# Attention and a gated feed-forward on one core: the softmax sums of 14 head pairs formed by accumulating transfers

## The chip, the cores and the metric

The kernel runs on one core of a Trainium2 chip. The time is the device time of one execution in microseconds, on that core; before the change it is 910.99 us, the median of three runs (910.42 to 911.65). TensorE (PE) does matrix products, VectorE (DVE) and ScalarE (ACT) work element by element, GpSimd (POOL) here clears two tiles and issues transfers, SyncE (SP) only issues transfers. SBUF is the on-chip memory of 128 partitions, PSUM the one that TensorE writes.

## The reference

Four batches of eight heads, 768 positions, head width 64. A query sees the keys with the same six hash bits; the result is laid out as 3,072 tokens of width 512 and goes through a feed-forward block of width 2,048.

```python
q_bits = (np.einsum('bhsd,dk->bhsk', q, proj) > 0)
k_bits = (np.einsum('bhsd,dk->bhsk', k, proj) > 0)
mask = q_bucket[:, :, :, None] == k_bucket[:, :, None, :]
scores = np.where(mask, scale * np.matmul(q, k.transpose(0, 1, 3, 2)), -1000000000.0)
attn = np.exp(scores - np.max(scores, axis=-1, keepdims=True))
attn = attn / (np.sum(attn, axis=-1, keepdims=True) + 1e-09)
x = np.matmul(attn, v)          # then (B,H,S,D) -> (B*S, H*D)
h = x @ w_in
g = h * erf(np.maximum(h, 0.0) + np.log1p(np.exp(-np.abs(h))))
out = g @ w_out
```

The sum over the keys in the fifth line is what the change treats. The weights w_in and w_out arrive as 64-bit floats, and the kernel makes 32-bit ones of them.

## The kernel before, in words

There are two stages. In the attention, two heads make a pair, so there are 16 pairs (i), each of two halves (h = 2i, 2i+1) of 384 queries. A half has six blocks of 128 keys. For a block, TensorE forms the scores of both heads with the keys on the partitions (`score`, L548: a product of hash bits that carries a large negative number where buckets differ, then q and k); ScalarE takes exp into `e_all` (L566), which holds nine blocks; TensorE multiplies by v (`weigh`, L629). Three PSUM tiles hold scores, so TensorE can be three blocks ahead of ScalarE.

The sum of e over the keys is made in two steps. VectorE adds the six blocks of a half (`sum_keys`, L617), in two wide rooms (`wide_sums`: x_sum and blocks[1], tiles that are free until the feed-forward), alternating by halves. That leaves 128 partial sums for each query, one on each partition. TensorE adds these with a matrix of ones (`divisor`, L664, tile z_ps), ScalarE copies the row out (`keep_divisor`, L677). For a pair, SP then sends z to DRAM and gets it back spread over the partitions (`spread`, `gather`), VectorE inverts it (`invert`), SP sends it out and broadcasts it back (`ungather`, `widen`, tile r), VectorE multiplies (`normalise`, L750), and SP stores the pair (`send`).

The hash bits of pair i are computed some pairs ahead: TensorE (`bits_of`, L817), sign on ScalarE (`sign_of`, L826), a weight on VectorE (`weigh_bits`, L836), and then POOL sends them to DRAM (`leave_bits`, L846) and, once they have landed, brings them into the layout that the scores need (`place_bits`, L855, two transfers).

Beside this the weights are converted, in 32 pieces of 128 x 512: POOL loads a piece of 512 KB (`fetch_weights`, L454, tile raw), ScalarE makes a mask of it (`square_high`, `keep_normal`), VectorE makes the high part (`move_bits`, `mask_bits`), the rest (`add_rest`, L522), and adds both (L530). Eight sums of weight blocks (`presum_weights`, L771, tile w_sum) prepare the feed-forward, which uses Strassen-like products.

The order of all this is made by a planner in the kernel, `arrange`. Each operation is given an engine, a cost, a rank, what must come before it (`after`), and `late`, the time from its end until another engine may count on it. The planner keeps a clock for each engine and emits, again and again, the operation that starts first, by rank. TensorE's order is a chain fixed by hand. The planner's clock sets the order only; at run time each engine works off its own list in that order, and waits on semaphores. An instruction that waits holds back all that stand behind it on its engine. In the planner before, what follows on the same engine is counted as ready when its predecessor ends, which for a transfer is when it was issued.

Of the kernel before, what the change touches and what calls it, by code (L numbers as in the profile page):

```python
# [54 lines left out]
F32 = mybir.dt.float32  # L55
BF16 = mybir.dt.bfloat16
I32 = mybir.dt.int32
# [6 lines left out]
P = 128  # L64
# [22 lines left out]
class Op:  # L87
# [11 lines left out]
    table: str = None  # L99
    late: float = 0.06  # L100


# [15 lines left out]
def arrange(ops, rooms, patience=0.0):  # L118
# [18 lines left out]
    def open_up(op):  # L137
        at = 0.0
        for a in op.after:
            if a in names:  # L140
                away = 0.0 if names[a].engine == op.engine else names[a].late
                at = max(at, ready[a] + away)
        open_ops[op.engine].append((op, at))
# [50 lines left out]
def kernel(  # L194
# [36 lines left out]
    QB = QR // 2  # L231
    WARM = 10
    proj_sb = const.tile([P, 2 * QR], F32, name="proj_sb")
    weight = const.tile([P, 2], F32, name="weight")
# [179 lines left out]
    def attention():  # L414
        NS = NPAIR * 4
        with (
# [10 lines left out]
            def big(name):  # L427
# [9 lines left out]
            raws = {}  # L437
            NH = NPAIR * 2
            wide_sums = [
                t.rearrange("p a b c -> p (a b c)")[:, 0 : 4 * HS].rearrange(  # L440
# [36 lines left out]
            def move_bits(n):  # L477
                if n not in raws:
                    return
                high = raws[n][:, :, 1]  # L480
                top = raws[n, "top"] = cvt.tile([P, WP], I32, name="top", tag="top")
# [16 lines left out]

            def mask_bits(n):
                if n not in raws:  # L500
                    return
                top = raws[n, "top"]
                unit = raws[n, "unit"] = cvt.tile([P, WP], I32, name="unit", tag="unit")
# [12 lines left out]
            def add_rest(n):  # L516
                if n not in raws:
                    return
                top, unit = raws.pop((n, "top")), raws.pop((n, "unit"))
                low = raws.pop(n)[:, :, 0]  # L520
                rest = cvt.tile([P, WP], F32, name="rest", tag="rest")
                nc.vector.scalar_tensor_tensor(  # L522
                    out=rest,
                    in0=low.bitcast(U32),
                    scalar=2.0**-52,
                    in1=unit[:, :].bitcast(F32),
                    op0=ALU.mult,
                    op1=ALU.mult,
                )
                nc.vector.tensor_tensor(  # L530
                    out=pieces[n][0], in0=top[:, :].bitcast(F32), in1=rest, op=ALU.add
                )
# [60 lines left out]
            def sum_keys(h, k):  # L593
                i, half = divmod(h, 2)
                d = pairs[i]
                if k == 0:
                    if h >= NH - 2:
                        if half:
                            room = blocks[1][:, :, :].rearrange("p k t -> p (k t)")[:, 0:S]
                        else:  # L600
                            room = load.tile([P, S], F32, name="q", tag="q")
                        d["sum", half] = room.rearrange("p (n a c) -> p n a c", n=1, a=2)
                    else:
                        d["sum", half] = wide_sums[h % 2]
                s = d["sum", half]
# [31 lines left out]
            def home(i, what):  # L637

                if i < NPAIR - 1:
                    shape, bufs = {"x": (S, 3), "z": (HS, 1), "r": (S, 2)}[what]  # L640
                    return xst.tile([P, shape], F32, name=what, tag=what, bufs=bufs)
# [48 lines left out]
            def leave_plain(i):  # L690
# [9 lines left out]
                )  # L700

            def spread(i):

# [25 lines left out]
            def ungather(i):  # L729
                d = pairs[i]  # L730
                rd = d["rd"] = dram.tile([2, 2, HS], F32, name="rd", tag="rd")
                nc.sync.dma_start(
                    out=rd.rearrange("h a c -> (h a c)").rearrange("(p c) -> p c", c=2 * S // P),
                    in_=d["zc"],
                )
# [108 lines left out]
            def leave_bits(i):  # L844
                bd = pairs[i]["bd"] = dram.tile([4, 2, QB, HS], BF16, name="bd", tag="bd")
                nc.gpsimd.dma_start(out=bd.rearrange("n a r c -> (n a r) c"), in_=sg)  # L846

            def place_bits(i):
# [30 lines left out]
            for h in range(NH):  # L879
# [3 lines left out]
                if h % 2 and (h + 3) // 2 < NPAIR:  # L883
                    order.append(("bits", (h + 3) // 2))
                if h >= 1:
                    order.append(("divisor", h - 1))
                order += [("weigh", 2 * h), ("weigh", 2 * h + 1)]
            slots = []
            for what, n in order:
# [12 lines left out]
                else:  # L902
                    h = n // 2
                    after = (("exponential", n, GC - 1),)
                    if n % 2 == 0:
                        after += (("leave", h - 1), ("leave_plain", (h - 1) // 2))
                    pe(weigh, (n,), 2.02, after)
            sums_after = {}
            for h in range(NH):
# [16 lines left out]
            for h in range(NH):  # L926
                for k, (blocks_, _, _, where) in enumerate(sum_steps(h)):
                    after = tuple(("exponential", 2 * h + b // GC, b % GC) for b in blocks_)
                    after += (("sum_keys", h, k - 1), ("sum_keys", h - 1, last_sum(h - 1)))
                    if k == 0:  # L930
                        after += (("divisor", h - 2),)
                        if h == NH - 2:
                            after += (("measure", NPAIR - 3, 0, 1),)
                    op(sum_keys, (h, k), "DVE", 1.72 if where == 2 else 0.92, (1, 2 * h + 1, k), after)
            for h in range(NH - 1):
                i = h // 2
# [8 lines left out]
            for h in range(NH):  # L945
                i = h // 2
                op(leave, (h,), "ACT", 0.48, (0, 2 * h, -2), (("weigh", 2 * h + 1), ("send", i - 3)))
                if h % 2 == 0:
                    op(leave_plain, (i,), "DVE", 0.15, (0, 2 * h, 0), (("weigh", 2 * h + 1),))
            for i in range(NPAIR):  # L950
                n = 4 * i
                if i:
# [38 lines left out]
                if i == NPAIR - 1:  # L991
                    continue
                op(spread, (i,), "SP", 0.4, (0, n, 0), (("keep_divisor", 2 * i + 1),), late=3.0)
                op(gather, (i,), "SP", 0.35, (0, n, 1), (("spread", i),), late=4.5)
                op(invert, (i,), "DVE", 0.4, (0, n + 8, 3), (("gather", i),))
                op(ungather, (i,), "SP", 0.35, (0, n, 2), (("invert", i),), late=3.0)
                op(
# [12 lines left out]
            for n in range(len(pieces)):  # L1010
# [13 lines left out]
                op(mask_bits, (n,), "DVE", 1.1, (2, n, 1), (("move_bits", n), ("keep_normal", n)), late=1.5)  # L1024
                op(add_rest, (n,), "DVE", 1.3, (2, n, 2), (("mask_bits", n),))
            for k in range(8):
                op(
                    presum_weights,
                    (k,),
                    "DVE",  # L1030
                    1.2,
                    (2, 31, k),
                    (("add_rest", 8 * (k // 4) + 7), ("presum_weights", k - 1)),
                )
            op(load_x, (0,), "SP", 1.1, (1, 0), (("send", JP - 1), ("start_pair", 10)), late=4.0)
# [748 lines left out]
```

## Time and profile before

The profiled execution took 910.96 us, of which its span, from the first to the last instruction, is 909.2; TensorE's granted clock was 0.999.

| stage, us from the start | length | PE busy | DVE busy | ACT busy | DMA share |
|---|---|---|---|---|---|
| 20 to 50 | 30 | 29.97 | 28.84 | 25.07 | 0.48 |
| 50 to 80 | 30 | 28.63 | 26.79 | 23.05 | 0.69 |
| 110 to 140 | 30 | 30.00 | 28.98 | 23.15 | 0.74 |
| 200 to 230 | 30 | 30.00 | 28.04 | 25.57 | 0.50 |
| 290 to 320 | 30 | 30.00 | 28.44 | 21.85 | 0.25 |
| 321.58 to 909.20 (feed-forward) | 587.62 | 581.42 | 380.35 | 317.75 | 0.20 |

Busy times are microseconds in that stretch; the DMA share is the mean busy share of the core's 16 DMA engines. Instructions that issue transfers aren't counted as busy on SP and ACT. A profile line such as "L664 PE MATMUL z_ps<-x,ones" names the line of the kernel, the engine, the operation, the tile written and those read.

### The profile page before, as it was taken

Reading aid. Unit: us, or ns where it says so; the run is one execution under the profiler, and the core shown is the slowest. Engines: PE = TensorE matmul, PEld = TensorE weight load, DVE = VectorE, ACT = ScalarE, POOL = GpSimd, SP = SyncE. Lnnn points to the kernel's source line nnn. Section 1 sums busy time; section 2 is a strip of 40 time slices with the busy share of each in tenths; the row PEclk is TensorE's granted clock in tenths of the full one; section 3 lists DMA queues with packets and bytes.
Section 4 is the critical chain, followed back from the end, with each engine's and each line's share of the span. In section 5 each row is a group of like instructions: output and inputs, shape, how many; then the busy total and the mean of one; then the engine's idle time right before and its main releaser. Section 6 shows DMA issues by size and latency. Waiting matters only on the chain.

```text
span 909.2 us, 12885 instructions
## 1 busy us (share of the span) xinstructions
PE 900.3 (99%) x5016; PEld 661.9 (73%) x5016; DVE 673.3 (74%) x863; ACT 571.9 (63%) x824; POOL 58.2 (6%) x95
## 2 busy tenths in 40 slices
PE   9999999999999999999999999999999999999997
PEld 5444444444444478888888888888888888888886
DVE  5989999989999969986566556756776556655653
ACT  6878887888887849755555545555655555545520
POOL 0211111111121000000000001000100000000000
PEclk9999999999999999999999999999999999999999
DMA  8455677656574231111122114211321023101321
GB/s 203 130 162 148 169 176 189 187 141 165 157 194 136 59 123 64 38 45 70 52 65 82 35 47 105 81 36 47 87 99 35 35 58 94 35 32 52 69 70 50
DMA packets 65013, 86.83 MB, mean 96 GB/s; under 512 B 34348, under 2 KB 47500, under 8 KB 64944
## 3 DMA queue, kind: packets, MB, share of 16 engines
q1 hardware_dynamic: 56384, 63.81, 24.6%
q0 software_dynamic: 8112, 21.66, 8.6%
q8 instruction: 41, 0.67, 0.3%
q10 hardware_dynamic: 448, 0.46, 0.2%
q14 instruction: 28, 0.23, 0.1%
HBM read 64.67 MB, written 17.30 MB: 90 GB/s over the span
## 4 chain that ended last, share of the span: by engine, by line
PE 92%; issue 1%; DMA 1%; ACT 0%; POOL 0%; DVE 0%; DVEq 0%; ACTq 0%; POOLq 0%
PE M L1317 32%; PE X L1204 28%; PE st L548 14%; PE av L629 12%; PE M L1204 3%; PE z_ps L664 1%; PE bits L817 1%; DMA raw<-in_w_in_dram 0%; POOL both L855 0%; ACT e_all L566 0%; ACT keep L468 0%; DMA bd<-sg 0%; DVE u L1352 0%; ACT x L688 0%; DVEq L1727 0%
## 5 line engine op out<-in xcount | busy, mean ns | idle before, releaser
L1244 DVE SCALAR_TENSOR_TENSOR e<-w,e 128x1024 f32<-128x1024 f32 x144 | 173.8, 1221 | 8.9 <-ACT w L1238 4.2
L566 ACT ACTIVATE e_all<-st 128x768 f32<-128x768 f32 x192 | 150.9, 813 | 11.9 <-PE st L548 11.5
L1238 ACT ACTIVATE w<-h,cq 128x1024 f32<-128x1024 f32 x144 | 155.6, 1137 | 0.2 <-DVE e L1244 0.2
L548 PE MATMUL st<-q,k 64*128 64x384 f32 x768 | 155.0, 483 | 0.0
L1226 DVE TENSOR_TENSOR h<-X,h 128x512 f32<-128x512 f32 x65 | 44.8, 689 | 146.0 <-PE X L1204 145.8
L1317 PE MATMUL M<-w_out_sb,h 128*128 128x256 f32 x576 | 141.5, 379 | 0.0
L629 PE MATMUL av<-e_all,v 128*64 128x385 f32 (+1 forms) x768 | 131.1, 490 | 0.0
L1204 PE MATMUL X<-x,w_in_sb 128*128 128x256 f32 x512 | 121.0, 379 | 0.0
L1317 PEld LDWEIGHTS M<-w_out_sb,h 128*128 128x128 f32 x576 | 109.4, 190 | 14.9
L1222 ACT COPY h<-X 128x512 f32<-128x512 f32 x85 | 49.3, 580 | 112.4 <-PE X L1204 112.3
L1234 ACT ACTIVATE e<-h,cq 128x1024 f32<-128x1024 f32 x48 | 55.2, 1150 | 82.7 <-DVE h L1226 82.7
L1204 PEld LDWEIGHTS X<-x,w_in_sb 128*128 128x128 f32 x512 | 97.3, 190 | 13.2
L629 PEld LDWEIGHTS av<-e_all,v 128*64 128x64 f32 x768 | 52.4, 136 | 67.2 <-issue 65.2
L1317 PE MATMUL M<-wt,S 128*128 128x256 f32 x384 | 95.6, 379 | 0.0
L548 PEld LDWEIGHTS st<-q,k 64*128 64x128 f32 x768 | 68.2, 188 | 34.9 <-issue 34.2
L1204 PE MATMUL X<-x_sum,w_sum 128*128 128x256 f32 x344 | 81.3, 379 | 0.0
L1317 PEld LDWEIGHTS M<-wt,S 128*128 128x128 f32 x384 | 73.0, 190 | 9.9
L1204 PEld LDWEIGHTS X<-x_sum,w_sum 128*128 128x128 f32 x344 | 65.4, 190 | 8.9
L548 PE MATMUL st<-both 64*128 64x384 bf16 x384 | 62.9, 324 | 1.6 <-ACT e_all L566 1.4
L1259 DVE TENSOR_TENSOR h<-h,e 128x1024 f32<-128x1024 f32 x48 | 58.0, 1221 | 3.7 <-ACT e L1255 3.6
L1255 ACT ACTIVATE e<-e 128x1024 f32<-128x1024 f32 x48 | 50.4, 1054 | 7.8 <-DVE e L1244 7.4
L548 PEld LDWEIGHTS <-both 64*128 64x128 bf16 x384 | 19.5, 94 | 43.1 <-issue 21.2
(126 smaller groups left out, 1073.4 us busy)
## 6 DMA issues: line engine op xcount, KB each, us to landing
wt<-wt SPq DMA_DIRECT2D x24, 768.0 KB, 4.2
raw<-in_w_out_dram POOLq DMA_DIRECT2D x16, 512.0 KB, 4.6
raw<-in_w_in_dram POOLq DMA_DIRECT2D x14, 512.0 KB, 4.3
v<-in_v_dram SPq DMA_DIRECT2D x32, 192.0 KB, 4.8
xs<-x SPq DMA_DIRECT2D x16, 384.0 KB, 3.1
q<-in_qkT_dram SPq DMA_DIRECT2D x30, 192.0 KB, 4.2
k<-in_qkT_dram SPq DMA_DIRECT2D x30, 192.0 KB, 4.4
r<-rd SPq DMA_DIRECT2D x30, 192.0 KB, 3.4
```

Source lines behind the costliest of these rows:

```text
L548: nc.tensor.matmul(out=st[:, ab, 0:HS], lhsT=d["k" + src][rows, keys], rhs=d["q" + src][rows, cols], start=(part == 0), stop=(part == 1),)
L566: nc.scalar.activation(out=e[:, :, 0:HS], in_=st[:, :, 0:HS], func=AF.Exp, scale=scale)
L629: nc.tensor.matmul(out=d["av"][rows, 0:w], lhsT=d["v"][:, g * GC + c, rows], rhs=e[:, ab, 0:w], start=(g == 0 and c == 0), stop=(g == 1 an ...
L1204: nc.tensor.matmul(out=d[where][:, u, :], lhsT=a[:, kc, f : f + P], rhs=b[:, kc, :], start=(first and u == 0 and kc == 0), stop=(last and ...
L1222: nc.scalar.copy(out=quarter(p, q), in_=st[p][where])
L1226: nc.vector.tensor_tensor(out=h, in0=st[p][where], in1=h, op=ALU.add)
L1234: nc.scalar.activation(out=s, in_=unit(p, v), func=AF.Sigmoid, bias=cq[:, n : n + 1])
L1238: nc.scalar.activation(out=q, in_=unit(p, v), func=AF.Sigmoid, scale=GATE_S[j][0], bias=cq[:, j : j + 1])
L1244: nc.vector.scalar_tensor_tensor(out=s, in0=st[p].pop(("q", v, j)), scalar=GATE_S[j][2], in1=s, op0=ALU.add, op1=ALU.mult,)
L1255: nc.scalar.activation(out=s, in_=s, func=AF.Tanh, scale=GATE_LEAD)
L1259: nc.vector.tensor_tensor(out=h, in0=h, in1=st[p].pop(("s", v)), op=ALU.mult)
L1317: nc.tensor.matmul(out=banks[name][:, sub, :], lhsT=a[:, u, sub * P : (sub + 1) * P], rhs=b[:, u, :], start=(c == 0 and k == 0), stop=(c = ...
```

## The change

For the first 14 pairs (`FOLDED`), z no longer goes through TensorE. VectorE's last sum of each half writes into one of three rooms, `pair_sums` (parts of blocks[1] and of w_sum), both halves of a pair beside each other. POOL then issues three accumulating transfers one after another (`fold`): rows 64 to 127 are added to rows 0 to 63, then 32 to 63 to 0 to 31, then 16 to 31 to 0 to 15. SP stores the 16 rows that are left (`spread_folded`) and brings them back with 16 values beside each other (`gather_folded`, tile zr), VectorE adds these 16 and inverts (`invert_folded`). The last two pairs go the old way.

The new field `far` makes the planner count `late` for followers on the same engine too, so it leaves 6.0 us between one fold's issue and the next. The last addition of a weight piece also becomes an accumulating transfer of POOL's (`complete_weights`). The bits' transfers are issued by ScalarE. The weight sums that write into w_sum wait until pair_sums no longer need that room. The old z path's own tile goes, its stored pairs get four buffers instead of three.

```diff
-                away = 0.0 if names[a].engine == op.engine else names[a].late
+                near = names[a].engine == op.engine and not names[a].far
+                away = 0.0 if near else names[a].late
...
+            FOLDED = NPAIR - 2
+            pair_sums = [
+                t.rearrange("p a b -> p (a b)")[:, 0 : 2 * S]
+                for t in (blocks[1][:, :, :], w_sum[:, 2, :, :], w_sum[:, 1, :, :])
+            ]
...
             def add_rest(n):
...
                 nc.vector.scalar_tensor_tensor(
-                    out=rest,
+                    out=unit,
                     in0=low.bitcast(U32),
                     scalar=2.0**-52,
-                    in1=unit[:, :].bitcast(F32),
+                    in1=unit,
                     op0=ALU.mult,
                     op1=ALU.mult,
                 )
-                nc.vector.tensor_tensor(
-                    out=pieces[n][0], in0=top[:, :].bitcast(F32), in1=rest, op=ALU.add
+
+            def complete_weights(n):
+
+                if (n, "unit") not in raws:
+                    return
+                nc.gpsimd.dma_start(
+                    out=pieces[n][0],
+                    in_=raws.pop((n, "unit"))[:, :].bitcast(F32),
+                    accum_op=ALU.add,
                 )
...
+                if i < FOLDED and k == last_sum(h):
+                    into = pair_sums[i % 3][:, half * S : (half + 1) * S].rearrange(
+                        "p (n a c) -> p n a c", n=1, a=2
+                    )
...
+            def fold(i, k):
+
+                n = P >> (k + 1)
+                s = pair_sums[i % 3]
+                nc.gpsimd.dma_start(out=s[0:n, :], in_=s[n : 2 * n, :], accum_op=ALU.add)
...
+            def spread_folded(i):
+
+                zf = pairs[i]["zf"] = dram.tile([ROWS, 2 * S], F32, name="zf", tag="zf")
+                nc.sync.dma_start(out=zf, in_=pair_sums[i % 3][0:ROWS, :])
+
+            def gather_folded(i):
+                d = pairs[i]
+                zr = d["zr"] = small.tile([D, ROWS, 2 * S // D], F32, name="zr", tag="zr", bufs=1)
+                nc.sync.dma_start(
+                    out=zr, in_=d.pop("zf").rearrange("r (p c) -> p r c", c=2 * S // D)
+                )
+
+            def invert_folded(i):
+                d = pairs[i]
+                zc = d["zc"] = small.tile([D, 2 * S // D], F32, name="zc2", tag="zc2")
+                nc.vector.tensor_reduce(
+                    out=zc, in_=d.pop("zr").rearrange("p r c -> p c r"), axis=AX.X, op=ALU.add
+                )
...
             def leave_bits(i):
                 bd = pairs[i]["bd"] = dram.tile([4, 2, QB, HS], BF16, name="bd", tag="bd")
-                nc.gpsimd.dma_start(out=bd.rearrange("n a r c -> (n a r) c"), in_=sg)
+                nc.scalar.dma_start(out=bd.rearrange("n a r c -> (n a r) c"), in_=sg)
...
-                    nc.gpsimd.dma_start(
+                    nc.scalar.dma_start(
                         out=both[i % 2][ab * D : ab * D + NBIT + 1, :, :].rearrange(
...
-                if h >= 1:
+                if h - 1 >= 2 * FOLDED:
                     order.append(("divisor", h - 1))
...
-                op(leave, (h,), "ACT", 0.48, (0, 2 * h, -2), (("weigh", 2 * h + 1), ("send", i - 3)))
+                op(leave, (h,), "ACT", 0.48, (0, 2 * h, -2), (("weigh", 2 * h + 1), ("send", i - 4)))
...
-                        op(leave_bits, (i,), "POOL", 0.7, (0, n - 6, 2), (("weigh_bits", i),), late=3.6)
+                        op(leave_bits, (i,), "ACT", 0.65, (0, n - 6, 2), (("weigh_bits", i),), late=5.0, far=True)
                         op(
                             place_bits,
                             (i,),
-                            "POOL",
-                            1.2,
+                            "ACT",
+                            1.25,
                             (0, n - 6, 3),
                             (("leave_bits", i), ("score", n - 5, 2), ("clean", i - 2)),
-                            late=3.6,
+                            late=4.5,
                         )
...
+                if i < FOLDED:
+                    for k in range(FOLDS):
+                        before = ("fold", i, k - 1) if k else ("sum_keys", 2 * i + 1, last_sum(2 * i + 1))
+                        op(fold, (i, k), "POOL", 0.9, (0, n, 4 + k), (before,), late=LATE, far=True)
+                    op(spread_folded, (i,), "SP", 0.4, (0, n, 0), (("fold", i, FOLDS - 1),), late=3.0, far=True)
+                    op(gather_folded, (i,), "SP", 0.35, (0, n, 1), (("spread_folded", i),), late=4.5, far=True)
+                    inverse = invert_folded
+                    op(inverse, (i,), "DVE", 0.7, (0, n + 8, 3), (("gather_folded", i),))
...
-                op(add_rest, (n,), "DVE", 1.3, (2, n, 2), (("mask_bits", n),))
+                op(add_rest, (n,), "DVE", 0.7, (2, n, 2), (("mask_bits", n), ("complete_weights", n - 2)))
+                op(complete_weights, (n,), "POOL", 0.9, (0, n, 1), (("add_rest", n),), late=5.5)
+            before = ()
+            for n, k in enumerate((0, 1, 2, 4, 5, 6, 3, 7)):
+                after = tuple(("complete_weights", 8 * (k // 4) + m) for m in range(8))
+                if k % 2:
+                    after += (("spread_folded", FOLDED - (1 if k % 4 == 3 else 3)),)
+                op(presum_weights, (k,), "DVE", 1.2, (2, 31, n), after + before)
+                before = (("presum_weights", k),)
```

More of the change, by code (lines that the diff above doesn't have):

```diff
@@ L100 @@
     late: float = 0.06
+    far: bool = False
 TABLE_LOAD = 1.28
@@ L232 @@
     WARM = 10
+    FOLDS = 3
     proj_sb = const.tile([P, 2 * QR], F32, name="proj_sb")
@@ L480, in move_bits @@
                 high = raws[n][:, :, 1]
-                top = raws[n, "top"] = cvt.tile([P, WP], I32, name="top", tag="top")
+                top = raws[n, "top"] = pieces[n][0].bitcast(I32)
                 nc.vector.tensor_scalar(
@@ L502, in mask_bits @@
                 top = raws[n, "top"]
-                unit = raws[n, "unit"] = cvt.tile([P, WP], I32, name="unit", tag="unit")
+                unit = raws[n, "unit"] = cvt.tile([P, WP], I32, name="unit", tag="unit", bufs=2)
                 nc.vector.scalar_tensor_tensor(
@@ L518, in add_rest @@
                     return
-                top, unit = raws.pop((n, "top")), raws.pop((n, "unit"))
+                raws.pop((n, "top"))
+                unit = raws[n, "unit"][:, :].bitcast(F32)
                 low = raws.pop(n)[:, :, 0]
-                rest = cvt.tile([P, WP], F32, name="rest", tag="rest")
                 nc.vector.scalar_tensor_tensor(
-                    out=rest,
+                    out=unit,
                     in0=low.bitcast(U32),
                     scalar=2.0**-52,
-                    in1=unit[:, :].bitcast(F32),
+                    in1=unit,
                     op0=ALU.mult,
@@ L603, in sum_keys @@
                     else:
-                        d["sum", half] = wide_sums[h % 2]
+                        d["sum", half] = wide_sums[h % 2 if i >= FOLDED else 0]
                 s = d["sum", half]
@@ L639, in home @@
                 if i < NPAIR - 1:
-                    shape, bufs = {"x": (S, 3), "z": (HS, 1), "r": (S, 2)}[what]
-                    return xst.tile([P, shape], F32, name=what, tag=what, bufs=bufs)
+                    if what == "z":
+                        return x_sum[:, :, :, :].rearrange("p a b c -> p (a b c)")[:, S : S + HS]
+                    return xst.tile([P, S], F32, name=what, tag=what, bufs={"x": 4, "r": 2}[what])
                 rows = blocks[1][:, :, :].rearrange("p k t -> p (k t)")
@@ L700, in leave_plain @@
                 )
+            def fold(i, k):
+                n = P >> (k + 1)
+                s = pair_sums[i % 3]
+                nc.gpsimd.dma_start(out=s[0:n, :], in_=s[n : 2 * n, :], accum_op=ALU.add)
+            ROWS = P >> FOLDS
+            LATE = 6.0
+            def spread_folded(i):
[13 more added lines that the diff above has]
+                )
+                nc.vector.tensor_scalar(
+                    out=zc, in0=zc, scalar1=S * EPS, scalar2=None, op0=ALU.add
+                )
+                nc.vector.reciprocal(out=zc, in_=zc)
             def spread(i):
@@ L732, in ungather @@
                 nc.sync.dma_start(
-                    out=rd.rearrange("h a c -> (h a c)").rearrange("(p c) -> p c", c=2 * S // P),
+                    out=rd.rearrange("h a c -> (h a c)").rearrange(
+                        "(p c) -> p c", c=2 * S // (D if i < FOLDED else P)
+                    ),
                     in_=d["zc"],
@@ L907, in attention, with i_of @@
                     pe(weigh, (n,), 2.02, after)
+            def i_of(h):
+                return h // 2
             sums_after = {}
@@ L930, in attention @@
                     if k == 0:
-                        after += (("divisor", h - 2),)
+                        if h == NH - 3:
+                            after += (("spread_folded", FOLDED - 2),)
+                        if h - 2 >= 2 * FOLDED:
+                            after += (("divisor", h - 2),)
                         if h == NH - 2:
                             after += (("measure", NPAIR - 3, 0, 1),)
+                    if k == last_sum(h) and i_of(h) < FOLDED:
+                        after += (("spread_folded", i_of(h) - 3),)
                     op(sum_keys, (h, k), "DVE", 1.72 if where == 2 else 0.92, (1, 2 * h + 1, k), after)
-            for h in range(NH - 1):
+            for h in range(2 * FOLDED, NH - 1):
                 i = h // 2
@@ L992, in attention @@
                     continue
[L993 to L996, printed above, removed]
+                if i < FOLDED:
[6 more added lines that the diff above has]
+                    op(inverse, (i,), "DVE", 0.7, (0, n + 8, 3), (("gather_folded", i),))
+                else:
+                    op(spread, (i,), "SP", 0.4, (0, n, 0), (("keep_divisor", 2 * i + 1),), late=3.0, far=True)
+                    op(gather, (i,), "SP", 0.35, (0, n, 1), (("spread", i),), late=4.5, far=True)
+                    inverse = invert
+                    op(inverse, (i,), "DVE", 0.4, (0, n + 8, 3), (("gather", i),))
+                op(ungather, (i,), "SP", 0.35, (0, n, 2), ((inverse.__name__, i),), late=3.0, far=True)
                 op(
@@ L1024, in attention @@
                 op(mask_bits, (n,), "DVE", 1.1, (2, n, 1), (("move_bits", n), ("keep_normal", n)), late=1.5)
-                op(add_rest, (n,), "DVE", 1.3, (2, n, 2), (("mask_bits", n),))
[L1026 to L1034, printed above, removed]
+                op(add_rest, (n,), "DVE", 0.7, (2, n, 2), (("mask_bits", n), ("complete_weights", n - 2)))
[7 more added lines that the diff above has]
+                before = (("presum_weights", k),)
             op(load_x, (0,), "SP", 1.1, (1, 0), (("send", JP - 1), ("start_pair", 10)), late=4.0)
```

## The prediction, made before the change was run

> **What bounds the kernel now.** I read the page first (busy shares, the 40 slices), then the chain of waits over one pair, then the busy time by stage, then the tiles of the hash bits.
>
> ```profile
> PE 900.3 (99%) x5016; PEld 661.9 (73%) x5016; DVE 673.3 (74%) x863; ACT 571.9 (63%) x824; POOL 58.2 (6%) x95
> PE   9999999999999999999999999999999999999997
> DVE  5989999989999969986566556756776556655653
> ACT  6878887888887849755555545555655555545520
> DMA  8455677656574231111122114211321023101321
> ```
>
> TensorE is busy for all but 9 us. In the first 14 slices (22.7 us each), the attention, VectorE and ScalarE are nearly full too and the DMA digits stand at 4 to 8; after that three of the four have room. So the attention is the stage to argue from, and it ends where the first feed-forward matmul starts, at 321.58 us in the chain. One pair of heads in that chain:
>
> ```profile
> 90.94 4.95 PE st L548 x36
> 95.89 0.46 PE z_ps L664 x8
> 96.36 4.03 PE av L629 x24
> 100.39 4.95 PE st L548 x36
> 105.34 0.78 PE bits L817 x8
> 106.12 0.33 PE z_ps L664 x8
> 106.45 4.02 PE av L629 x24
> 110.47 4.95 PE st L548 x36
> ```
>
> From 90.94 to 110.47 is 19.53 us a pair, with no hole: 2 x (4.95 + 4.02), 0.78 for the bits, and 0.46 + 0.33 for the two z products, which the change takes out. The same stretch, ten pairs long, by engine:
>
> ```profile
> core 0: us, PE busy (x) PEld busy (x) DVE busy (x) ACT busy (x) POOL busy (x), PEclk, DMA share, GB/s
> 80.86:276.15 195.29, 195.29 (x1442) 90.86 (x1444) 183.98 (x245) 158.52 (x290) 28.31 (x50) 1.00 0.64 169
> 112.00:114.00 2.00, 2.00 (x18) 1.25 (x16) 1.97 (x4) 2.00 (x4) 0.42 (x1) 1.00 0.98 261
> ```
>
> The reader is to see three reserves. DVE: 18.40 us of 19.53, practically none. ACT: 15.85 of 19.53. DMA: 0.64 x 19.53 = 12.5 us of all 16 engines a pair; in the loads' burst (the last row) it is already full, at 261 GB/s.
>
> **What the Trainium skill says.** "DMA: Bandwidth & Descriptors", section "SWDGE vs HWDGE vs iDMA": only GpSimd can issue an accumulating transfer, so folds and weight sums share POOL's queue with the weight loads. The trace agrees as far as it goes: its only accumulating transfers (u<-part, w<-part) are POOL's. The same page, "Issuing engines are not separate DMA queues": transfers issued by SP, ACT and POOL run on the same 16 engines. So moving the bits' transfers to ScalarE frees POOL's time and not a byte of bandwidth. The burst row above fits that: SP's loads and POOL's transfers together reach 0.98. "VectorE: DVE Perf Modes", section "The perf-mode tier table": tensor_reduce has only the 1x mode; no row here shows one.
>
> **The change part by part**, against the profiled run's own 910.96 us (span 909.2 and 1.8 around it); the median of 910.99 is the same number.
>
> *z off TensorE (28 of 32 halves).* Removes 0.46 + 0.33 = 0.79 us a pair; if a z beside the bits costs the full 0.46, 0.92. 14 pairs: 11.1 to 12.9, taken 12. The path is TensorE without a hole, so this comes through whole unless something else ends a wait. What would be late next are the DMA, ScalarE and VectorE, below.
>
> *z off ScalarE.* Two copies z<-z_ps at 0.33: 0.65 a pair, off the path.
>
> *VectorE.* Goes: one of the three-instruction finish of a weight piece, L530 at 0.692, two pieces a pair: 1.38. Comes: a reduce of 64x384 read elements, bounded by a 384-wide bf16 multiply (0.32) and a 512-wide f32 add (0.69), taken 0.5, and 0.05 for the wider reciprocal. Net -0.8. Seven of the eight weight presums (1.22 each) wait until pair_sums leave w_sum, so 8.5 us go from the middle to the last five halves: 18.40 - 0.8 - 1.0 = 16.6 a pair in the middle, while the last 20 us (19.41 of 20.48 busy) get fuller. Covered by the first 30 us of the feed-forward, where DVE has 7.6 us free; without that cover up to 5 us at its start.
>
> *New DMA work.* An accumulating 256 KB transfer has its price in the feed-forward:
>
> ```profile
> 555.60:561.50 5.90, 5.90 (x29) 5.20 (x28) 5.19 (x7) 2.13 (x4) 1.72 (x2) 1.00 0.66 133
> 561.60:567.00 5.40, 5.40 (x26) 4.75 (x25) 0.23 (x1) 0.59 (x1) 0.00 (x0) 1.00 0.29 97
> ```
>
> The second row holds 512 KB of plain stores: 0.29 x 5.4 = 1.57 us of 16 engines, 0.78 per 256 KB. The first holds one such store and two accumulations: 0.66 x 5.9 = 3.89, less 0.78, halved: 1.55 us each, twice the plain price. Per pair the change adds two weight sums (3.1), folds of 384 + 192 + 96 KB (2.6 x 1.55 = 4.1), zf of 96 KB (0.3), and zr, 1,024 rows of 96 bytes, of which no row shows the like (0.3 by bytes, perhaps 1; taken 0.6), less 0.1 for zd and zc: 8.0. With today's 12.5 that is **20.5 us of DMA a pair, where TensorE would need only 18.7**. 12.5 is measured in crowded bursts. At a quiet load's rate (a stretch from 106 to 108 us, raw alone, shows 0.65 at 224 GB/s, so 345 per full share) the 169 GB/s x 19.53 us = 3.3 MB cost 9.6, and the sum is 17.6. So 17.6 to 20.5, middle 19.0; the loads have deadlines, and I let the engines be used to 0.95: 20.1 us a pair.
>
> *POOL.* Goes: bits 0.55 + 2 x 0.58. Comes: five accumulations at 0.85 to 1.0. About +3 us a pair of 28.31/10; not the bound. But a fold waits in POOL's queue for the fold before, planned 6.0 us, and behind it stand the weight loads and sums. One transfer of 256 KB landed in 3.8 to 5.2 us on an idle DMA; the first fold is larger and goes off while the next pair's loads do. If it takes longer than 6.0, raw is late, and ScalarE waits for raw in order. The z path gets longer by some 20 us of planned time; four x buffers (74 us of pairs) hold that.
>
> *The bits on ScalarE.* Three issues a pair: 0.34 (SP's rows) to 0.6 (ACT's first loads, 1.20 for two): 1.0 to 1.8, taken 1.4. New are ScalarE's own waits: leave_bits for VectorE's weighed bits, place_bits for the landing.
>
> ```profile
> L826 ACT ACTIVATE sg<-bits,sgn x14: 586/591/638, 26.7 to 282.1; 128x384 bf16<-128x384 f32 x14
> L836 DVE TENSOR_SCALAR sg<-sg,weight_q x14: 319/320/321, 28.8 to 284.9; 64x384 bf16<-64x384 bf16 x14
>   POOL bd L846: 82.2, 14
> DMA to landing us min/median/max: 1.9/3.5/6.4
> ```
>
> POOL waited 82.2 us for these bits and nobody minded, for POOL had nothing behind them. Behind ScalarE stand the exps. In the timelines VectorE finishes the bits 1.6 to 4.6 us after the sign (mean 3.4), mostly since it works off its queue late. What ScalarE does in between is copies and squares, so its wait is between 0 and 3.4 a pair; VectorE's own relief shortens it, taken 1. The landing is planned at 5.0, median 3.5, longest 6.4: mostly covered now, less in a fuller DMA. ScalarE: 15.85 - 0.65 + 1.4 + 1 = 17.6 of 18.7 to 20.1. It fits on average; at the 20.1 us a pair that the DMA sets it has 2.5 us to spare.
>
> **Sum.** 14 pairs from 19.53 to 20.1 us: +8; the rest as before: 910.96 + 8 = **919 us**.
>
> **The rivals.**
> - *A, the forecast: the 16 DMA engines become the bound*, 919. For it: 20.5 against 18.7, and that the chain of z now has eight transfers, all in the crowd. Against: bursts are smoothed by three load buffers and 6 us between a load's landing and its use.
> - *B, the other side: the transfers stay under cover.* Place: the same DMA engines; price: 17.6 us a pair at quiet rates, under TensorE's 18.7; it decides from a DMA share under about 0.95 on, with ScalarE's bits waits within its 3.7 us of idle time. Then only z's removal counts: 910.96 - 12 = 899. For it: TensorE ran without a hole through 30 us stretches of 0.74.
> - *C, ScalarE's in-order waits replace the removed z.* Wait 2 us, issues 1.4, copies -0.65: 2.75 more a pair, in the weigh phase that already has no ScalarE idle time (0.21 us before the copy of av, against 2.37 in the other half). The three score banks absorb some 0.7; TensorE loses 2.0: 18.7 + 2.0 = 20.7, 14 x 1.2 = +17: 928. Against: VectorE is relieved.
> - *D, gain and stalls cancel*: 911. For it: the middle of the DMA sum, 19.0, with some waits, is 19.5.
>
> **How the numbers follow.** A 0.36, B 0.34, C 0.22, D 0.08. What can be told from no change is about 0.2%, 1.8 us. Faster 0.34 (B), same 0.08 (D), slower 0.58 (A and C). The range: low end B with a small rest of stalls at its ideal, 898; high end beyond C with some of A's crowding, 934. A alone: 912 (19.6 us a pair) to 927 (20.7).
>
> **What would show it.** Right: DMA share in the attention above 0.9, pairs at about 20 us, holes in TensorE before scores or bits whose releaser is a transfer (bits, loads) or an exp behind raw; fold landings above 6 us. Wrong: share below 0.85 and st to st in 18.7 us (B); or ACT waits of 2 us at leave_bits with a half-empty DMA (C). A feed-forward longer than its 587.6 us would say that the moved presums weren't covered, which no case here holds.

## The result, and the profile after

The changed kernel takes 977.12 us (median of four runs, 975.22 to 981.23), where the kernel before took 910.80 in the same comparison: a ratio of 1.0733, with a 95% interval of 1.0697 to 1.0769. The forecast was 919 with a range from 898 to 934: slower is right, the size is not.

The page of the profiled execution (981.23 us, span 979.4), its busy shares and slices of 24.5 us:

```profile
PE 914.6 (93%) x4792; PEld 669.3 (68%) x4792; DVE 667.2 (68%) x845; ACT 559.0 (57%) x796; POOL 97.2 (10%) x127
PE   9998878887979896999999999999999999999997
DVE  5886765776678689799766656665566566666653
ACT  6876654655666583596555555555555556555630
PEclk9999998898989999899999999999999999999999
DMA  7888876798879765211113201320132013001311
```

TensorE has 224 instructions less and yet holes in the attention; VectorE and ScalarE, nearly full before, have room now; the DMA digits stand mostly at 7 to 9 as far as the attention goes. No engine is full there and the transfers nearly are, which suggests that engines wait for landings; the waits below show it.

By stages: the first feed-forward matmul starts at 382.46 us, where it stood at 321.51, so 61 of the span's 70.2 us are lost in the attention. From there to the end it is 596.9 us against 587.7: 9.2 more. In the other cut, TensorE is idle for 64.8 us instead of 8.9 (span less busy), and busy for 14.3 more although z's products went: the score products take 171.7 + 70.0 us instead of 155.0 + 62.9, at a granted clock of 0.84 to 0.94 in most 30 us stretches with holes. Their larger group, before and after:

```profile
L548 PE MATMUL st<-q,k 64*128 64x384 f32 x768 | 155.0, 483 | 0.0
```

```profile
L563 PE MATMUL st<-q,k 64*128 64x384 f32 x768 | 171.7, 525 | 0.0
```

The Trainium skill ("TensorE: Matmul & The Clock Gate", "Part 1: The HAM clock gate") says why: "the default state is throttled, and activity releases the throttle". Both the holes and the lower clock in their stretches are in the trace. In the pair shown below, the clock reads 0.50 from 147 to 151 us, right after a hole of 4.68 us, and 1.00 from 152 us on; the scores of a block take 1.60 us there instead of 0.81. The products with v, which come later in a pair, take what they took (131.6 us, before 131.1). By these numbers the lower clock added about 24 us of slower products to the 56 us more of holes.

Who waited for whom, in the changed kernel's list of waits (total, times, longest):

```profile
ACT junk L669 <- DVE sg L891: 55.6, 14, 7.8
POOL w_sum L726 <- DMA w_sum<-w_sum: 53.1, 12, 7.3
PE st L563 <- ACT e_all L581: 43.2, 19, 6.1
DVE zc L747 <- DMA zr<-zf: 37.9, 11, 7.1
```

Read from the bottom up, it is one story, and one pair shows it in the timeline. VectorE:

```profile
131.30 1.75 DVE L636 TENSOR_TENSOR x_sum<-e_all 128x1536 f32<-128x1536 f32 x1
138.47 1.09 DVE L747 TENSOR_REDUCE zc<-zr 64x24 f32<-64x384 f32 x1 [5.42 <-DMA zr<-zf]
139.60 0.17 DVE L750 TENSOR_SCALAR zc<-zc 64x24 f32<-64x24 f32 x1
139.81 0.29 DVE L753 RECIPROCAL zc<-zc 64x24 f32<-64x24 f32 x1
140.03 1.69 DVE L636 TENSOR_TENSOR x_sum<-x_sum,e_all 128x1536 f32<-128x1536 f32 x1
141.75 0.96 DVE L636 TENSOR_TENSOR w_sum<-x_sum 128x768 f32<-128x768 f32 x1
142.74 0.32 DVE L891 TENSOR_SCALAR sg<-sg,weight_q 64x384 bf16<-64x384 bf16 x1
```

ScalarE in the same stretch:

```profile
137.01 0.51 ACT L669 ACTIVATE junk<-q 128x384 bf16<-128x384 f32 x1
137.42 0.19 ACT L669 ACTIVATION_READ_ACCUMULATOR junk<-q 128x1 f32 x1
143.09 0.35 ACTq L901 DMA_DIRECT2D bd<-sg  x1
143.49 0.52 ACT L669 ACTIVATE junk<-q 128x384 bf16<-128x384 f32 x1 [5.88 <-DVE sg L891]
```

And TensorE:

```profile
141.59 0.81 PE L563 MATMUL st<-q,k 64*128 64x384 f32 x4
147.09 0.50 PE L563 MATMUL st<-both 64*128 64x384 bf16 x2 [4.68 <-ACT e_all L581]
```

The inversion of an earlier pair stands in VectorE's list and its zr is still on its way: 5.42 us. Behind it are two sums and then this pair's weighed bits. ScalarE has come to leave_bits, which issues these bits, and stands for 5.88 us. Behind leave_bits are the copy of av and the next exps. TensorE fills its three banks of scores and stands for 4.68. A landing that is 5 us late is paid by three engines in turn, and in this pair comes out as a hole of almost the same length. Before the change VectorE waited 2.0 us for zc in the whole execution.

### The profile page after: what moved, and what is told of

Read it like the earlier page. It is cut to its first block, busy times and chain, and to the rows that moved or that the text cites. A ratio compares the mean times of both kernels' runs of the same rounds, so it can differ in the third digit from the quotient of the medians.

```text
span 979.4 us, 12421 instructions
## 1 busy us (share of the span) xinstructions
PE 914.6 (93%) x4792; PEld 669.3 (68%) x4792; DVE 667.2 (68%) x845; ACT 559.0 (57%) x796; POOL 97.2 (10%) x127
## 4 chain that ended last, share of the span: by engine, by line
PE 68%; DMA 16%; DVE 7%; issue 3%; ACT 2%; SPq 2%; POOL 0%; ACTq 0%; DVEq 0%; POOLq 0%
PE M L1389 30%; PE X L1276 26%; DMA zr<-zf 6%; PE st L563 4%; PE M L1276 4%; DMA zf<-w_sum 3%; PE av L648 3%; DVE x_sum L636 3%; DMA zf<-x 2%; DMA r<-rd 2%; DVE zc L747 1%; DMA w_in_sb<-unit 1%; DMA w_sum<-w_sum 1%; ACT e_all L581 1%; SPq L364 1%
## 5 line engine op out<-in xcount | busy, mean ns | idle before, releaser
L581 ACT ACTIVATE e_all<-st 128x768 f32<-128x768 f32 x192 | 145.2, 815 | 49.4 <-DMA q<-in_qkT_dram 12.7
L563 PE MATMUL st<-q,k 64*128 64x384 f32 x768 | 171.7, 525 | 0.0
L648 PE MATMUL av<-e_all,v 128*64 128x385 f32 (+1 forms) x768 | 131.6, 491 | 2.6 <-ACT x L708 2.6
L563 PE MATMUL st<-both 64*128 64x384 bf16 x384 | 70.0, 347 | 48.4 <-ACT e_all L581 43.2
L563 PEld LDWEIGHTS st<-q,k 64*128 64x128 f32 x768 | 76.3, 204 | 29.1 <-issue 27.6
L563 PEld LDWEIGHTS <-both 64*128 64x128 bf16 x384 | 25.3, 98 | 102.6 <-issue 72.7
L636 DVE TENSOR_TENSOR x_sum<-e_all 128x1536 f32<-128x1536 f32 x29 | 50.8, 1751 | 14.6 <-ACT e_all L581 14.5
```

What stands on the lines that cost most here:

```text
L563: nc.tensor.matmul(out=st[:, ab, 0:HS], lhsT=d["k" + src][rows, keys], rhs=d["q" + src][rows, cols], start=(part == 0), stop=(part == 1),)
L581: nc.scalar.activation(out=e[:, :, 0:HS], in_=st[:, :, 0:HS], func=AF.Exp, scale=scale)
L648: nc.tensor.matmul(out=d["av"][rows, 0:w], lhsT=d["v"][:, g * GC + c, rows], rhs=e[:, ab, 0:w], start=(g == 0 and c == 0), stop=(g == 1 an ...
```

## The experiments

Where it helps, I give the mean time from one pair to the next, from the start of the first sign of the hash bits to that of the last, 13 pairs: 19.65 us before, 24.0 in the changed kernel.

**First: take away one part of the change at a time.** Bits on POOL again:

```diff
-                nc.scalar.dma_start(out=bd.rearrange("n a r c -> (n a r) c"), in_=sg)
+                nc.gpsimd.dma_start(out=bd.rearrange("n a r c -> (n a r) c"), in_=sg)
...
-                        op(leave_bits, (i,), "ACT", 0.65, (0, n - 6, 2), (("weigh_bits", i),), late=5.0, far=True)
+                        op(leave_bits, (i,), "POOL", 0.7, (0, n - 6, 2), (("weigh_bits", i),), late=3.6, far=True)
```

> The hash bits' three transfers a pair are issued by POOL again, with the planned costs of before; all else as in the changed kernel (977 us). If ScalarE's own in-order waits (leave_bits behind VectorE's weighed bits, place_bits' issue) are what cost the time, 930 to 945. If the late z path (VectorE waiting in order for zr) is the root and ScalarE only hands that wait on, 970 to 985, since POOL's queue then holds the bits behind folds that land after 7 to 9 us.

Measured: 942.8 us, ratio 1.0363 (1.0337 to 1.0388), as expected for ScalarE's own waits. So 34 us hang on which engine issues three small transfers a pair, although VectorE's wait for zr is nearly as long as it was (30.0 us). What is left runs close to the limit of the 16 DMA engines. The stretch from 80 to 300 us, first in the changed kernel, then here (columns: PE, PEld, DVE, ACT, POOL busy, granted clock, DMA share, GB/s):

```profile
80.00:300.00 220.00, 179.94 (x1095) 84.04 (x1096) 149.96 (x199) 129.08 (x235) 47.73 (x62) 0.90 0.82 185
```

```profile
80.00:300.00 220.00, 199.49 (x1280) 92.70 (x1280) 174.35 (x229) 156.29 (x272) 75.06 (x102) 0.96 0.97 215
```

At a share of 0.97 and 21.4 us a pair (304.91 less 27.19, over 13), 20.8 us of DMA are done a pair. The prediction's sum was 20.5.

The weights' last addition on VectorE again:

```diff
-                nc.gpsimd.dma_start(
-                    out=pieces[n][0],
-                    in_=raws.pop((n, "unit"))[:, :].bitcast(F32),
-                    accum_op=ALU.add,
-                )
+                nc.vector.tensor_tensor(
+                    out=pieces[n][0],
+                    in0=pieces[n][0],
+                    in1=raws.pop((n, "unit"))[:, :].bitcast(F32),
+                    op=ALU.add,
+                )
```

> The last addition of a weight piece is VectorE's again (32 accumulating transfers of 256 KB less, 32 additions of 0.69 us more); the folds and the bits on ScalarE stay. If the 16 DMA engines' volume is the bound, 3.1 us of them less a pair, 935 to 950. If the z path's latency against its place in VectorE's order is the root, 960 to 975, as each transfer of the path lands only a little earlier.

Measured: 969.36 us (ratio 1.0644, 1.0626 to 1.0662): about a seventh of the volume (3.1 of 20.5 us a pair) taken away gives 8 us, while VectorE gets its additions back. So this part of the volume isn't what holds the changed kernel; ScalarE still waits 41.0 us for the bits.

The planner is told the times that transfers take here:

```diff
-            LATE = 6.0
+            LATE = 9.0
...
-                    op(spread_folded, (i,), "SP", 0.4, (0, n, 0), (("fold", i, FOLDS - 1),), late=3.0, far=True)
-                    op(gather_folded, (i,), "SP", 0.35, (0, n, 1), (("spread_folded", i),), late=4.5, far=True)
+                    op(spread_folded, (i,), "SP", 0.4, (0, n, 0), (("fold", i, FOLDS - 1),), late=8.0, far=True)
+                    op(gather_folded, (i,), "SP", 0.35, (0, n, 1), (("spread_folded", i),), late=8.0, far=True)
```

> The planner is told what the transfers really take: 9.0 us for a fold, 8.0 for zf and for zr (6.0, 3.0 and 4.5 in the changed kernel), with six ev tiles so that the longer path has room. The transfers themselves are the same. If VectorE's early place for the inversion is the root, its wait for zr goes and the time falls to 915 to 935. If the volume is the bound, 960 to 980, with the waits moved elsewhere (loads, raw).

Measured: 944.79 us (ratio 1.0379, 1.0361 to 1.0398), 32 less, with the same transfers, but above the 915 to 935 expected. Two lines of its waits:

```profile
ACT junk L669 <- DVE sg L891: 8.0, 9, 1.4
ACT x L708 <- DMA xs<-x: 40.3, 10, 5.8
```

VectorE's wait for zr is gone from the list, and ScalarE's wait for the bits fell from 55.6 to 8.0 us: it came from VectorE's early place for the inversion, not from VectorE's load. The new wait is for a free x tile, since pairs are now stored later; it was not expected, and it keeps this run from telling more.

The folds left out:

```diff
-                        op(fold, (i, k), "POOL", 0.9, (0, n, 4 + k), (before,), late=LATE, far=True)
+                        pass
...
-                    op(spread_folded, (i,), "SP", 0.4, (0, n, 0), (("fold", i, FOLDS - 1),), late=3.0, far=True)
+                    op(spread_folded, (i,), "SP", 0.4, (0, n, 0), (("sum_keys", 2 * i + 1, last_sum(2 * i + 1)),), late=3.0, far=True)
```

> The three folds are left out (the divisor then sums 16 of the 128 partial rows); zf, zr, weight sums by transfer and bits on ScalarE stay. It takes away 4.1 us of DMA a pair and some 24 us of the z path's length. Both the volume theory and the latency theory expect 900 to 925; if ScalarE's waits for the bits or the weight sums by transfer are the root, it stays above 940.

Measured: 941.23 us (ratio 1.0332, 1.0315 to 1.0349), above what two of the theories expected. VectorE still waits 24.7 us for zr and ScalarE 42.7 for the bits, at a DMA share of 0.71 to 0.79. So zf, zr and the weights' transfers suffice to break the plan without any fold, when ScalarE issues the bits: zr, planned at 4.5 us, stands in the chain of waits with 7 to 9 us a pair.

**Second: one part alone, the rest as before.** Three kernels with the edits above; in the last two, z is TensorE's for all pairs (FOLDED = 0, z in its own tile, three x tiles).

> Folds alone: bits on POOL and the weights' last addition on VectorE as before, the z path by folds for 14 pairs. If what is left over at 943 us with the bits on POOL is the DMA volume (share 0.94 to 1.01 there), 3.1 us of 20.5 a pair less take the share to about 0.85 and the time to 912 to 925. If it is the z path's length against VectorE's order, 930 to 942, with VectorE still waiting some 30 us for zr.

> The bits' transfers on ScalarE alone: z on TensorE for all pairs, the weights' last addition on VectorE. If ScalarE's wait for the weighed bits is a cost of its own, VectorE being as late as before (1.6 to 4.6 us after the sign), 925 to 945. If ScalarE only hands on waits that the late z path makes, 909 to 915.

> The weights' accumulating transfers alone: z on TensorE for all pairs, bits on POOL. DMA goes from 12.5 to 15.6 us a pair, VectorE has 1.4 us a pair less to do. Volume theory: share about 0.8, no bound yet, 908 to 914. If POOL's waits in front of the weight loads cost, 915 to 930.

Measured: folds alone 934.61 us (ratio 1.0265, 1.0248 to 1.0282); bits alone 911.89 (1.0011, 1.0004 to 1.0018); weights alone 913.03 (1.0028, 1.0012 to 1.0044); the last two lie in the lower of their ranges. ScalarE as the bits' issuer costs 1 us where the plan holds and 34 where it doesn't. Of the three, the folds are the part that costs alone. Their 934.6 lies in the range for the z path's length, but the wait that was to show it doesn't: the DMA share is 0.84 to 0.89 between 80 and 260 us and VectorE waits only 8.5 us for zr; TensorE waits for the bits (both<-bd, 21.8 us before weight loads and 14.6 before products), which POOL issues between its folds. What makes these bits late wasn't tried. The attention ends 13.7 us later than before, and the rest takes 9.5 us more.

**Third: folds that nobody waits for**, added to the kernel with the weights alone (there, too, seven of the eight weight sums then wait for the last fold, so they move from the middle to the end):

```diff
+                    if i < NPAIR - 2:
+                        for k in range(FOLDS):
+                            before = ("fold", i, k - 1) if k else ("sum_keys", 2 * i + 1, last_sum(2 * i + 1))
+                            op(fold, (i, k), "POOL", 0.9, (0, n, 4 + k), (before,), late=LATE, far=True)
                     op(spread, (i,), "SP", 0.4, (0, n, 0), (("keep_divisor", 2 * i + 1),), late=3.0, far=True)
```

> As f3_only_weights (z on TensorE, bits on POOL, weights by transfer: 913), and POOL also issues the three folds of each of 14 pairs, on a part of w_sum that was cleared and that nobody reads: their volume (4.1 us of DMA a pair) and their places in POOL's queue without any engine waiting for their results. If the volume or POOL's queue costs by itself, 925 to 945, with bits and raw late. If the folds cost only through those who wait for z, 912 to 918.

> As g3_idle_folds (934.6: folds that nobody waits for, weights by transfer, z on TensorE), but the bits' transfers are issued by ScalarE. If the idle folds cost through POOL's queue, in which the bits stood behind a fold waiting for the fold before, most of it goes: 912 to 920. If they cost through the volume on the 16 engines, 928 to 940, with share near 0.9 and loads late.

Measured: 934.58 us with bits on POOL (ratio 1.0291, 1.0246 to 1.0337) and 953.63 with bits on ScalarE (1.0492, 1.0456 to 1.0529). The stretch from 80 to 300 us without the idle folds (f3_only_weights), then with them (g3_idle_folds):

```profile
80.00:300.00 220.00, 220.00 (x1626) 102.77 (x1624) 190.27 (x252) 179.47 (x328) 52.49 (x79) 1.00 0.76 191
```

```profile
80.00:300.00 220.00, 209.14 (x1516) 97.76 (x1514) 171.35 (x232) 166.13 (x305) 76.74 (x105) 0.99 0.93 217
```

At a share of 0.76 TensorE has no hole at all; at 0.93 it has 11 us of them here. So the folds cost some 22 us though nobody uses their result: 17 in the attention, which ends at 336.91 us instead of 319.69, and 5 behind it, where the moved weight sums now stand. Three lines of the waits with bits on POOL show how:

```profile
DVE zc L778 <- DMA zc<-zd: 37.4, 13, 8.6
POOL bd L902 <- DVE sg L892: 24.9, 9, 6.3
PE st L564 <- DMA both<-bd: 9.8, 8, 4.4
```

The longest of each follow one another: VectorE stands 8.6 us for zc, POOL then 6.3 for the weighed bits, TensorE then 4.4 for the bits' landing. The landing of zc, 6 KB, takes 4.1 us from its issue (median), where it took 1.6 before and 2.6 with the weights alone; VectorE's wait for it was 2.0 and 18.6 us there. In this hole, and in the next longest (2.15 us, before which POOL stood 4.92), it isn't the folds in POOL's queue that hold the bits, for POOL was waiting for VectorE. The run with bits on ScalarE lies above both of its ranges. There the old z path's short transfers (zd and zc, planned at 3.0 and 4.5) stand in the chain with 4.5 to 8.0 us, VectorE waits 23.5 us for zc and ScalarE 29.9 for the bits. It is the changed kernel's story without any folded z. How much POOL's queue adds in the other pairs can't be told from these two runs, since moving the bits also brings ScalarE's own waits.

**Fourth: what is z's removal worth?** The z path is cut behind the sums; folds, zf and zr go from the plan too (not shown here):

```diff
-                nc.vector.tensor_reduce(
-                    out=zc, in_=d.pop("zr").rearrange("p r c -> p c r"), axis=AX.X, op=ALU.add
-                )
+                nc.vector.memset(zc, 1.0)
```

> For 14 pairs the z path is cut: sums on VectorE as in the changed kernel, then no folds, no zf, no zr, and ones in place of the divisor; bits on POOL, weights on VectorE. It shows what taking z off TensorE is worth when nothing takes its place: 897 to 901 by the prediction's own term of 12 us. If VectorE is a bound of its own, above 905.

> As f4_no_z (z path cut, ones in place of the divisor, bits on POOL), but with the weights' last addition by accumulating transfer, so that VectorE has 1.4 us a pair less. If f4_no_z gained only 2.2 us because VectorE (55 to 57 us of 60) became the bound, this one shows more of the prediction's 12: 897 to 903. If TensorE's holes there have another cause (loads, raw), 906 to 912 again.

> As f4_no_z (908.7), but the planner counts on r 12.0 us after its issue instead of 6.5, so that VectorE doesn't stand at normalise while r is on its way. If the missing 10 us of the prediction's 12 went into that wait, 898 to 903. If VectorE's own work (55 to 57 of 60 us) is what holds TensorE there, 906 to 910, with the wait for r gone.

Measured, in this order: 908.72 us (ratio 0.9977, 0.9965 to 0.9989), 925.50 (1.0184, 1.0125 to 1.0243) and 907.58 (0.9970, 0.9960 to 0.9980). The middle one is a miss: with VectorE relieved by transfers, r lands in 8.2 us (planned 6.5), VectorE waits for it 14 times, 28.1 us in all, and TensorE has holes again. The last one answers. In its timeline eight pairs are 18.74 us apart, which is 19.53 less the 0.79 that the chain showed for z; one pair takes 21.83. Its attention ends at 314.17 us, 7.3 earlier than before. Then 4.1 us are given back: from there to the end it is 591.8 us. The stretch from 80 to 300 us:

```profile
80.00:300.00 220.00, 217.67 (x1486) 100.46 (x1484) 211.28 (x291) 179.66 (x317) 31.95 (x56) 1.00 0.63 165
```

VectorE is at 0.96 there. TensorE's two holes are in the long pair, 1.00 and 1.32 us, and end with the loads of q and k; SP issued these behind a transfer for which it had stood 10.3 us for VectorE's inversion, and VectorE has no gap of note from 205 to 245 us. Behind the attention TensorE waits 3.52 us for VectorE's h. So even if z cost nothing, 3.4 us would be gained, not 12. This points to a nearly full VectorE as the next bound, in the attention through SP's queue and again at the seam to the feed-forward; no run relieves VectorE without adding transfers.

**Fifth: the best plan for real folds.** Longer planned times (9.0 for a fold, 8.0 for zf and zr, 12.0 for r), weights on VectorE, bits on ScalarE, five x tiles; then with fewer pairs folded. Before these, the longer plan was tried with the whole volume and bits on POOL (r still planned at 6.5).

> All of the change with bits on POOL and the longer planned times of e3_plan_later, and with five x tiles and one r tile, so that ScalarE doesn't wait for a stored pair. The volume stays at 20.5 us a pair. Volume theory: no waits for zr, but still 932 to 945, with a share near 1.0. If e1 and e3 each took away one part of the same waits and nothing else binds, 905 to 925.

> Real folds, bits on ScalarE, the weights' last addition on VectorE (17.4 us of DMA a pair), and planned times of 9.0 for a fold, 8.0 for zf and zr, 12.0 for r, five x tiles, one r tile. If late plan plus volume is the whole cause, it is the best version with folds: 905 to 918. If it stays above 925, VectorE (its additions and 1.09 us for the reduce) or the volume binds even so.

> As h3_folds_replanned (934.5), but 11 pairs are folded instead of 14, z has its own tile for the others, one unit tile. In h3 the attention ended earlier than before (318.5 against 321.5 us) and the span from there on was 611.5 us against 587.7, as VectorE stood for the last folded pairs' r in front of the feed-forward's work. If that seam is all that is left, 905 to 914; if the crowd of transfers binds in the attention too, 915 to 925.

> As i1_folds_11 with 8 pairs folded. If the seam was all: 907 to 912, 8 x 0.79 = 6.3 us less work on TensorE. If the crowd still costs more than z does, between i1 and before's 911 from above.

Measured, in this order: 940.33 us (ratio 1.0319, 1.0300 to 1.0339), 934.50 (1.0267, 1.0246 to 1.0287), 925.01 (1.0146, 1.0129 to 1.0163) and 920.46 (1.0103, 1.0086 to 1.0120). The first fits the range for the volume as the bound, 932 to 945, but not for that reason. With the whole volume the DMA share is 0.93 to 1.05 between 80 and 260 us (by this measure it can come out above 1), a pair takes 20.3 us, and the attention ends at 330.99 us, 9.5 later than before. The other 22 us are lost behind it, where the DMA share of the first 30 us is 0.39 and TensorE stands twice:

```profile
340.30 6.18 PE L1276 MATMUL M<-x_sum,w_sum 128*128 128x256 f32 x16 [5.59 <-issue]
362.15 3.78 PE L1276 MATMUL M<-x_sum,w_in_sb 128*128 128x256 f32 x8 [11.56 <-DVE h L1298]
```

With less volume (14 pairs, weights on VectorE, h3_folds_replanned) the attention is 3 us shorter than before (318.48 us), and the loss is all at the seam, 23.8 us. VectorE there:

```profile
333.95 0.68 DVE L343 TENSOR_TENSOR x_sum<-x,x_sum 128x512 f32<-128x512 f32 x1
337.78 1.02 DVE L806 SCALAR_TENSOR_TENSOR x<-x,ev,r 128x768 f32<-128x768 f32 x1 [3.15 <-DMA r<-rd]
343.37 1.02 DVE L806 SCALAR_TENSOR_TENSOR x<-x,ev,r 128x768 f32<-128x768 f32 x1 [4.57 <-DMA r<-rd]
344.31 0.68 DVE L1362 TENSOR_TENSOR wt<-w_out_sb 128x512 f32<-128x512 f32 x1
```

And TensorE:

```profile
335.37 1.89 PE L1277 MATMUL M<-x,w_sum 128*128 128x256 f32 x8
350.71 1.65 PE L1277 MATMUL M<-x_sum,w_in_sb 128*128 128x256 f32 x3 [13.46 <-DVE h L1299]
```

The normalisation of the last folded pairs stands in VectorE's list in front of the feed-forward's first additions, and r comes late. Folding 11 or 8 pairs makes the seam smaller, 14.3 and 5.0 us more than before's 587.7 by their profiles, but doesn't bring the time under before's; their attention ends 0.3 us earlier and 2.9 later than before's. By TensorE's work alone (0.79 us a pair) it should end 8.7 and 6.3 us earlier; why it doesn't was not taken apart. No version with folds beats the kernel before; the fewer pairs are folded, the nearer it comes.

## Why the prediction was right in sign and wrong in size

- *TensorE's path and the 0.79 us a pair for z*: right, and shown: 18.74 us a pair where nothing else binds. "So this comes through whole unless something else ends a wait" was priced at 12 us for the rival B; it is worth 3.4, as late loads of q and k behind a nearly full VectorE, and the seam, take the rest (h1_no_z_late_r).
- *The DMA sum, 20.5 us a pair*: right at its crowded end, with 20.8 done at a share of 0.97 (e1_bits_pool). The quiet price of 17.6 was no use in a stage that is crowded throughout. Its step to the time, 20.1 us a pair and +8 us, is borne out where the plan is later and POOL issues the bits: 20.3 us a pair and 9.5 us of the attention (g2_bits_pool_later). What that run loses beyond it lies behind the attention. In e1_bits_pool, where VectorE still waits 30.0 us for zr, a pair takes 21.4 and the attention 24.5 us more.
- *The step that failed*: "what ScalarE does in between is copies and squares, so its wait is between 0 and 3.4 a pair; VectorE's own relief shortens it, taken 1", and from it "It fits on average". The measured wait is 55.6 / 14 = 4.0, and it isn't covered: TensorE stands 43.2 us for exps, and its score products take 24 us more at the lower clock, for which the prediction had no term; together 4.8 us a pair, where the forecast let ScalarE's waits cost nothing and rival C took 2.0. The bound took VectorE's lateness from the kernel before, in which VectorE waits almost only for engines close by. In the changed kernel VectorE itself stands for zr, 37.9 us in 11 waits, a wait that the prediction never priced: it named the longer z path only for its need of x buffers and as an argument for A. With a later plan that wait goes, ScalarE's falls to 8.0 us, and the time by 32 (e3_plan_later).
- *A and C as rivals*: they don't compete, each makes the other worse. Late landings make VectorE stand, the bits on ScalarE hand its standing on to the exps, and TensorE's clock falls in the holes. The part C alone costs 1 us, A alone (bits on POOL) about 32, both 66. So "slower" was forecast for the volume, which with the later plan costs some 10 us in the attention; that the sign came out right is in part luck.
- *Landings*: zr was priced by its bytes for the engines, 0.3 to 1 us. Its time to landing is what counted: 7.0 us where the profile shows it (e1_bits_pool), planned 4.5.
- *The reduce*: 1.09 us, outside of the bounds of 0.32 and 0.69 taken from other operations. 0.6 us a pair.
- *"A feed-forward longer than its 587.6 us ... no case here holds"*: it is 596.9. In its timeline VectorE makes three of the moved weight sums between 387.0 and 391.4 us, within a hole of 6.69 us of TensorE's. What the late z of the last folded pairs adds is shown for h3_folds_replanned, not for this run.

## What to carry to other kernels

An order that is planned with transfer times holds only as long as the transfers land in time; in these runs added volume made most landings later, also those of transfers that it didn't touch (zc 1.6, 2.6 and 4.1 us at shares of 0.60, 0.76 and 0.93), and an in-order engine that waits for one of them passes its wait to everything behind it. So price new transfers twice: as a share of the 16 engines, and as later landings of the old ones against the places of their waiters. Don't give a transfer to an engine on the critical path if it must first wait for an engine that itself waits for transfers. And look at the seam to the next stage: a version whose attention was 3 us shorter lost 23.8 us there.

## What the runs showed of the hardware that I had not expected

Accumulating transfers with nothing waiting for them still cost: 4.1 us of engine time a pair by their price turned an attention that had no hole between 80 and 300 us into one that is 17 us longer. Issuing itself becomes long in the crowd. In the changed kernel the issues of the bits' placement on ScalarE:

```profile
L910 ACTq DMA_DIRECT2D both<-bd x28: 272/273/1727, 33.6 to 345.6; - x28
```

The median is 0.27 us and the longest 1.73, from 175.79 us on, at a DMA share of 1.09 between 175 and 178 us; the exp behind it starts at 177.56. With the bits alone on ScalarE (f2_only_bits), at a share of 0.62 from 80 to 300 us, the longest is 0.53. The strided sum over 16 values, 64 x 384 elements read, takes 1.09 us, more than the two operations that were to bound it (0.32 and 0.69):

```profile
L747 DVE TENSOR_REDUCE zc<-zr 64x24 f32<-64x384 f32 x14 | 15.3, 1090 | 37.9 <-DMA zr<-zf 37.9
```

How much of that is the stride and how much the operation wasn't tried.
